# Chunk-selected attention and a softplus layer on one core: the steps in another fixed list

## The chip, the cores and the metric

The kernel runs on one core of a Trainium2 chip. The metric is the device time in microseconds (us) of one execution. Engines: TensorE (PE; its weight loads are PEld), VectorE (DVE), ScalarE (ACT), GpSimd (POOL) and SyncE (SP, which issues most DMAs). Each works through its own instructions strictly in the order of the program, and waits where an input or a buffer is not ready.

## The reference

```python
k_chunks = k.reshape(B, H, nc, chunk, D)             # B=4, H=8, S=768, D=64, chunk=32, nc=24
k_min, k_max = k_chunks.min(3), k_chunks.max(3)
ub = sum_d(max(q * k_min, q * k_max))                # a bound for every query and chunk
ub = where(causal, ub, -1e9); top_chunks = argsort(ub)[..., -6:]
scores = q @ k.T / sqrt(D); masked to the six chosen chunks and to earlier positions
x = (softmax(scores) @ v) as [3072, 512]             # 4 batches of 768 tokens
out = softplus(x @ w_in) @ w_out                     # w_in [512, 2048], w_out [2048, 512]
```

## The kernel before

Everything is one list of 1344 steps, a string called `ORDER`. A loop over it calls one small function for each word, and each function issues its instructions at once, so the list fixes the order on every engine and on every DMA queue; nothing reorders it. A letter at a word's end (V, A, G) says whether VectorE, ScalarE or GpSimd does that copy or sum.

The attention is cut into 20 units of two heads. Units 0 to 3 are the four head pairs of batch 0 for its first 384 tokens, units 4 to 7 the same pairs for its other 384, units 8 to 19 the pairs of batches 1 to 3 with all 768 tokens. The words of a unit u, in the order in which they depend on each other:

- loads: `bk`, `bq`, `bv` (batch 0, in pieces), `Lk`, `Lq`, `Lv` (a whole pair); casts to bf16: `hk`, `hq`, `hv` and `ck`, `cq`, `cv`, `cr`
- transposes of k and q: `kt`, `qt` on TensorE for batch 0 (lines 295, 302), `fk`, `fq` by DMA for the others (line 286)
- selection: `rg` the least and greatest k of a chunk (two, line 309), `pk` packs them into a table (line 314), `qp`, `qn` the positive and negative part of q (lines 328, 330, 335), `U` the bounds (TensorE, lines 345 and 346), `Ua` adds the causal mask, `M` finds the eight greatest (lines 352, 359), `T` writes the row of the choice (two instructions, lines 367 and 368)
- `a` or `s` turns that row on TensorE (lines 376, 387), `ac` or `sc` copies it beside q into `Qaug` (lines 381, 391); `kr`, `qr` put k and q into `Kaug`, `Qaug` (lines 318, 322)
- `S` scores (line 426, `S8.1.2` is unit 8, head 1, third group of columns), `E` exponential on ScalarE (line 432), `D` the causal triangle on GpSimd (line 437), `V` the sum over the values (line 453), `n` divides (lines 463 to 469), `X`, `x` turn the result into `xT` (lines 475, 485)

The layer behind it works on halves of 384 tokens: `I` (line 495) multiplies by `w_in`, `P` is the softplus (line 499). The second product is `F` (line 507) for batch 0; for the others a block scheme with seven products: `g` forms sums of activations (line 551), `m` multiplies (line 565), `e` adds into the output (lines 573 to 585). `t` forms the sums of weights that the scheme needs (line 541), `w` loads the weights. `ob`, `O`, `o` write out. `spin` is a product of zeros whose result nobody reads (line 197); `tE` and `tP` are a one-row activation that makes ScalarE load the table of the exponential or of the softplus.

Buffers are few: two tiles of PSUM each for scores, `I` and `spin` (`ps_big`), for `ub`, turned rows and results (`ps_sm`), and for `kt`, `qt`, `F`, `m` (`ps_w`). Loaded q, k and v have two tiles each. A step that takes the third tile waits until the first has been read.

Of the kernel before, what the change touches and what calls it, by code (L numbers as in the profile page):

```python
# [34 lines left out]
kt4 spin2 X3 x3.V x2.A kr5.0.A I0.0.2.1 I0.0.2.0 P0.0.2 pk5.1.G w2 I0.0.3.1 U5 qt4 I0.0.3.0 hk1.1.G P0.0.3 I0.0.1.0
I0.0.1.1 P0.0.1 qp4.V rg4.0 rg4.1 pk4.0.V qn4 pk4.1.G U4 I0.0.0.1 I0.0.0.0 tP P0.0.0 kr4.0.V kr4.1.V cau1 kt6 kt7 Ua5
kr6.0.A I0.0.4.0 I0.0.4.1 I0.0.5.1 I0.0.5.0 P0.0.4 P0.0.5 kr7.0.V Ua4 M4 rg6.0 T4 rg7.0 rg6.1 pk6.0.V rg7.1 kr6.1.V
pk6.1.V I0.0.6.0 I0.0.6.1 a4.1 I0.0.7.1 I0.0.7.0 ac4.1.A P0.0.6 bv1.0.2 bq1.1.0 bq1.1.1 Lq9 bv1.0.1 Lk8 bv1.1.0
bv1.0.0 bv1.1.2 bv1.1.1 P0.0.7 hq1.1.V qt6 M5 kr7.1.V T5 a5.0 ac5.0.V a4.0 S4.1.1 qn6 qp6.V ac4.0.V a5.1 qt7 zs0
# [10 lines left out]
tP F0.5.0 F0.5.1 S8.0.0 F0.3.0 S8.1.1 F0.3.1 F0.5.2 F0.3.2 F0.3.3 E8.1.1 E8.0.0 S8.1.2 E8.1.2 F0.3.4 S8.0.2 F0.5.3 s9  # L50
S8.1.0 rg10.1 qp10.V sc9.0.V qp11.V pk11.1.A cv11.A pk10.0.A E8.1.0 E8.0.2 kr11.0.G kr10.0.G qr10.0.G kr10.1.V cv8.A
D8.0 pk11.0.G pk10.1.G qr10.1.G Lk12 Lk13 D8.1 F0.5.4 F0.5.5 F0.3.5 U10 sc9.1.V qn11 Ua10 M10 S8.0.1 F0.5.6 S9.0.1
E8.0.1 U11 V8.1 S9.0.0 T10 n8.1 Ua11 M11 E9.0.1 E9.0.0 F0.5.7 S9.1.0 F0.3.6 ob0.5.A E9.1.0 s10 S9.1.1 F0.3.7 V8.0
S9.0.2 E9.1.1 E9.0.2 ck12.G kr11.1.G T11 n8.0 sc10.0.V sc10.1.V qr11.0.G qr11.1.G ck13.G F0.2.0 S9.1.2 F0.2.1 s11
# [604 lines left out]
```

## Time and profile before

| | |
|---|---|
| median of 3 runs | 262.48 us (261.29 to 262.59) |
| profiled execution | 263.69 us, its span from first to last instruction 262.0 us |
| PE busy | 246.1 us, 94% of the span |
| DVE busy | 183.5 us, 70% |
| ACT busy | 176.4 us, 67% |
| POOL busy | 122.5 us, 47% |
| mean granted TensorE clock | 0.986 of full speed |

PE is the engine to look at first, since it is nearly always busy; what a change of order can win is the time in which PE stands still or works at a lower clock. A busy share of 70% does not say that an engine is idle in every stage, so the shares have to be read by stretches.

### The profile page before, as it was taken

Reading aid. Unit: us, or ns where it says so; the run is one execution under the profiler, and the core shown is the slowest. Engines: PE = TensorE matmul, PEld = TensorE weight load, DVE = VectorE, ACT = ScalarE, POOL = GpSimd, SP = SyncE. Lnnn points to the kernel's source line nnn. Section 1 sums busy time; section 2 is a strip of 40 time slices with the busy share of each in tenths; the row PEclk is TensorE's granted clock in tenths of the full one; section 3 lists DMA queues with packets and bytes.
Section 4 is the critical chain, followed back from the end, with each engine's and each line's share of the span. In section 5 each row is a group of like instructions: output and inputs, shape, how many; then the busy total and the mean of one; then the engine's idle time right before and its main releaser. Section 6 shows DMA issues by size and latency. Waiting matters only on the chain.

```text
span 262.0 us, 6544 instructions
## 1 busy us (share of the span) xinstructions
PE 246.1 (94%) x2576; PEld 176.0 (67%) x2576; DVE 183.5 (70%) x553; ACT 176.4 (67%) x236; POOL 122.5 (47%) x148
## 2 busy tenths in 40 slices
PE   7568998999998989999999999999999999999994
PEld 2247665775654657666688888756688887668883
DVE  4877588436798998799999997419787782012593
ACT  5557857996769978866798798967576742662300
POOL 4655513592636983724667575203089910018000
PEclk9977999999999999999999999999999999999999
DMA  6999998859999979889999969994724234200212
GB/s 150 219 193 178 223 195 171 134 75 236 184 207 226 163 153 189 194 130 244 216 241 213 182 143 146 234 190 82 161 42 93 83 75 99 80 4 0 80 63 100
DMA packets 119903, 39.23 MB, mean 150 GB/s; under 512 B 113728, under 2 KB 115776, under 8 KB 119872
## 3 DMA queue, kind: packets, MB, share of 16 engines
q1 hardware_dynamic: 116736, 34.62, 68.2%
q0 software_dynamic: 3136, 4.19, 9.6%
q8 instruction: 20, 0.33, 0.5%
q14 instruction: 11, 0.09, 0.1%
HBM read 27.26 MB, written 6.29 MB: 128 GB/s over the span
## 4 chain that ended last, share of the span: by engine, by line
PE 71%; DVE 12%; ACT 6%; DMA 4%; POOL 3%; issue 2%; SPq 1%; ACTq 0%; POOLq 0%; DVEq 0%
PE hp L495 26%; PE op L565 21%; PE sc L426 11%; PE o_ps L453 6%; DMA qf<-in_q_dram 4%; ACT attnT L432 3%; PE op L507 3%; DVE km L309 2%; DVE m L359 2%; POOL attnT L437 1%; PE spin L197 1%; DVE row L368 1%; ACT Kaug L222 1%; DVE vaug L269 1%; DVE Kaug L318 1%
## 5 line engine op out<-in xcount | busy, mean ns | idle before, releaser
L432 ACT ACTIVATE attnT<-sc 128x1024 bf16<-128x1024 f32 (+3 forms) x96 | 84.1, 917 | 16.0 <-PE sc L426 14.5
L495 PE MATMUL hp<-xT,w_in_sb 128*128 128x384 bf16 x512 | 86.9, 326 | 0.0
L499 ACT ACTIVATE gT<-hp 128x768 bf16<-128x768 f32 x64 | 51.8, 810 | 39.1 <-PE hp L495 39.0
L495 PEld LDWEIGHTS <-w_in_sb 128*128 128x128 bf16 x512 | 49.3, 98 | 31.0 <-issue 0.2
L426 PE MATMUL sc<-Qaug,Kaug 128*128 128x128 bf16 (+3 forms) x400 | 51.9, 259 | 2.6 <-ACT Qaug L381 1.3
L437 POOL TENSOR_SCALAR_AFFINE_SELECT attnT<-attnT 128x768 bf16<-128x768 bf16 (+1 forms) x40 | 31.2, 781 | 26.8 <-ACT attnT L432 24.4
L426 PEld LDWEIGHTS <-Kaug 128*128 128x128 bf16 x400 | 29.9, 99 | 13.4 <-issue 3.8
L565 PEld LDWEIGHTS <-gT 128*128 128x128 bf16 x288 | 27.4, 98 | 5.4 <-DVE ob L579 0.7
L309 DVE TENSOR_REDUCE km<-kT_sb 128x24 bf16<-128x768 bf16 x24 | 22.3, 945 | 10.1 <-DMA kT_sb<-kb 10.1
L565 PE MATMUL op<-w_out_sb,gT 128*128 128x256 f16 x216 | 28.8, 272 | 0.0
L453 PE MATMUL o_ps<-vaug,attnT 128*128 128x65 bf16 x672 | 26.7, 194 | 1.4 <-DVE vaug L269 1.3
L453 PEld LDWEIGHTS <-attnT 128*128 128x128 bf16 x672 | 25.1, 98 | 4.2 <-issue 1.8
L507 PE MATMUL op<-w_out_sb,gT 128*128 128x512 f16 x96 | 26.4, 379 | 0.0
L551 DVE TENSOR_TENSOR mixa<-gT 128x1024 bf16<-128x1024 bf16 x7 | 6.9, 981 | 14.5 <-ACT gT L499 14.4
L359 DVE MAX8 m<-ubm 128x8 f32<-128x8 f32 (+4 forms) x192 | 16.4, 159 | 0.5
L318 POOL COPY Kaug<-kT_sb 64x768 bf16<-64x768 bf16 x17 | 14.4, 855 | 4.2 <-DMA kT_sb<-kb 3.3
L551 POOL TENSOR_TENSOR mixb<-gT,mixa 128x1024 bf16<-128x1024 bf16 x2 | 4.4, 2222 | 24.1 <-DVE mixa L551 24.0
L469 DVE TENSOR_TENSOR on<-o_ps,rr 128x384 bf16<-128x384 f32 x24 | 13.4, 557 | 0.8
L197 PE MATMUL spin<-zeros 128*128 128x512 bf16 x32 | 11.2, 489 | 1.5 <-DVE zeros L194 1.3
L507 PEld LDWEIGHTS <-gT 128*128 128x128 bf16 x96 | 8.4, 98 | 4.5
L352 DVE TENSOR_TENSOR ubm<-ub,causal 128x288 f32<-128x288 f32 (+2 forms) x20 | 7.6, 378 | 3.8 <-PE ub L346 3.3
L314 POOL COPY kmm<-km 64x48 bf16<-64x48 bf16 (+1 forms) x15 | 3.6, 237 | 14.2 <-DVE km L309 13.0
(116 smaller groups left out, 368.4 us busy)
## 6 DMA issues: line engine op xcount, KB each, us to landing
out_dram<-ob SPq DMA_DIRECT2D x24, 256.0 KB, 2.5
qf<-in_q_dram SPq DMA_DIRECT2D x12, 384.0 KB, 4.7
kf<-in_k_dram SPq DMA_DIRECT2D x12, 384.0 KB, 4.8
vf<-in_v_dram SPq DMA_DIRECT2D x12, 384.0 KB, 4.9
...
```

Of the source, the lines that this page charges most:

```text
L197: PE.matmul(o, state[0]["zeros"][:, 0:128], state[0]["zeros"], start=True, stop=True)
L309: V.tensor_reduce(st["km2"][:, which, :], st["kT"].rearrange("d (c t g) -> d c t g", t=4, g=CH // 4), axis=AX.XY, op=(ALU.max, ALU.min)[wh ...
L318: COPY[eng](Ka(p, e)[D * (1 - e):D * (2 - e), t0 * 128:t1 * 128], st["kT"][e * D:(e + 1) * D, :])
L359: V.max(out=st["m8"][:, t, e, :], in_=st["ubm"][:, t, 0:max(8, 4 * (t0 + t + 1)), e])
L426: PE.matmul(sc[:, o:o + (z - a) * 128], Ka(p, e)[:, tj * 128:(tj + 1) * 128], Qa(p, e)[:, a * 128:z * 128], start=True, stop=True)
L432: A.activation(st["at", e][:, g * 1024:g * 1024 + n], st["sc", e, g][:, 0:n], ACT.Exp, scale=scale)
L437: G.affine_select(out=d, in_=d, compare_op=ALU.is_ge, fill=0.0, base=0, channel_multiplier=-1, pattern=[[0, n], [1, 128]])
L453: PE.matmul(o[:, t, :], st["at", e][:, a:a + 128], va[:, tj, e, :], start=(tj == 0), stop=(tj == t0 + t))
L495: PE.matmul(hps[b, h, s][:, n, 0:HALF], w_in_sb[:, dt, ft * 128:(ft + 1) * 128], xT[b][:, dt, h * HALF:(h + 1) * HALF], start=(dt == 0), s ...
L499: A.activation(gT[b, h][:, 2 * s:2 * s + 2, :], hps.pop((b, h, s))[:, :, 0:HALF], ACT.Softplus)
L507: PE.matmul(held[b, t], g[:, ft, c:c + 128], w_out_sb[:, ft, :], start=(ft == 0), stop=(ft == KFF - 1))
L565: PE.matmul(o, x[:, f], y[:, f], start=(f == 0), stop=(f == KH - 1))
```

## The change

Only `ORDER` is replaced. Both lists hold the same 1344 steps with the same units and sizes. The steps stand in other places, and 115 copies, casts and sums go to another engine than before: nine casts of loaded tensors leave ACT for DVE or POOL, and ten of the `g` sums go from POOL to DVE while five go the other way. Among the steps that run behind the first `I` of batch 1, DVE receives the casts `ck17`, `cv12`, `cv13` and `cr15`, the copies `kr17.0` and `kr17.1`, the sums `g4.1.0` and `g4.1.1`, the eviction `e1.1.0` and some small copies (`pk`, `qp`); it gives away `cr17`, `kr15.0`, `t3.0`, `g1.1.1` and some small copies, and `t1.0` stands earlier. The diff is 88 lines of names; its start and the places that are spoken of below:

```diff
-spin9 ident rm0.V bk0.0.1 augb bk0.0.0 bk0.0.2 hk0.0.V cau0 augm kt0 bk1.0.1 bq0.0.2 bq0.0.1 bq0.0.0 bq0.1.2 ar0.1.A
...
-kr3.1.V ac0.1.A S0.1.0 E0.1.0 a0.0 kt2 Ua1 M1 T1 kr2.1.A ac0.0.A qp2.V D0.1 ar2.1.G w0 a1.1 S0.0.0 a1.0 qt3 rg2.0
...
-P0.1.1 I0.1.3.0 I0.1.3.1 P0.1.3 I0.1.0.1 I0.1.0.0 pk9.0.A P0.1.0 kr8.0.G ck10.G kr8.1.G qn9 qp8.V kr9.1.V cq10.V
...
-S10.0.0 E9.1.2 ob0.3.A Lq13 Lv9 cv9.V D9.1 cq13.G D9.0 t1.1.G Lv10 F0.2.2 S10.0.1 E10.0.0 sc11.0.V V9.1 sc11.1.V
...
+spin9 bk0.0.1 bk0.0.2 bk0.0.0 augb augm ar3.1.G kmm spin2 rm0.G ar0.0.A rm1.V ident vones ar3.0.G bq0.0.2 bq0.0.1
...
+bk1.1.1 bq1.0.1 bv0.0.1 bq1.0.0 bk1.0.0 bq1.0.2 bq1.1.0 bk1.0.1 bv0.1.1 bk1.1.0 qt2 U1 a0.0 spin2 S0.1.0 qp2.A ac0.0.A
+kr3.1.V Ua1 M1 T1 kt2 S0.0.0 qn2 ar2.0.V E0.1.0 D0.1 ar2.1.G w0 a1.1 a1.0 qt3 spin2 rg2.1 ac1.0.A E0.0.0 ac1.1.A
+pk3.0.A rg2.0 pk2.1.A pk3.1.A D0.0 hv0.0.0.G S1.1.0 qp3.V kr2.0.V pk2.0.V U2 qn3 U3 spin2 spin2 Ua2 Ua3 M2 hq1.0.V T2
...
+pk9.0.A P0.1.0 I0.1.2.1 I0.1.2.0 Lq10 P0.1.2 tP ob0.1.A cq10.A I0.1.4.1 I0.1.4.0 P0.1.4 qr9.0.G qr9.1.G qr8.1.G Ua8 M8
...
+M11 T11 S9.1.0 ob0.5.A E9.0.0 E9.1.0 V8.0 S9.1.1 F0.2.0 S9.0.2 F0.2.1 F0.2.2 E9.1.1 Lv9 D9.1 sc10.1.V cv9.V n8.0
```

ScalarE, units 0 to 3 of batch 0, from the first copy of a turned row (`ac0.1`) on. Before:

```order
L381 COPY Qaug_97<-qa 128x384
L432 ACTIVATE attnT<-sc 128x768
L318 COPY Kaug_93<-kT 64x384
L381 COPY Qaug_96<-qa 128x384
L432 ACTIVATE attnT<-sc 128x768
L245 CAST vaug_110<-vf 128x6x64
L314 COPY kmm_107<-km_312 64x2x12
L381 COPY Qaug_98<-qa 128x384
```

The same engine in the changed kernel, from the same copy on:

```order
L381 COPY Qaug_97<-qa 128x384
L222 COPY Kaug_90<-aug 64x768
L328 ACTIVATE qpos<-qT 128x384
L381 COPY Qaug_96<-qa 128x384
L432 ACTIVATE attnT<-sc 128x768
L381 COPY Qaug_98<-qa 128x384
L432 ACTIVATE attnT<-sc 128x768
L381 COPY Qaug_99<-qa 128x384
```

The copy into `Qaug_96` (`ac0.0`) now stands before the first exponential (`E0.1.0`) instead of behind it, and the copies of unit 1 (`Qaug_98`, `Qaug_99`) stand around the second.

VectorE, the selection of unit 8, from a `kr` copy on. Before:

```order
L318 COPY Kaug_91<-kT_sb 64x768
L266 CAST qb<-qf 128x768
L352 TENSOR_TENSOR ubm<-ub,causal 128x288
L359 MAX m_1359<-ubm 128x8 x12
L367 TENSOR_TENSOR row_113<-m_1359,minus 128x12
L368 TENSOR_TENSOR row_113<-ubm,m_1359 128x12x24
```

In the changed kernel:

```order
L318 COPY Kaug_90<-kT_sb 64x768
L309 TENSOR_REDUCE km_1327<-kT_sb 128x24 x2
L314 COPY kmm_105<-km_1327 64x48
L352 TENSOR_TENSOR ubm<-ub,causal 128x288
L359 MAX m_1367<-ubm 128x8 x12
L309 TENSOR_REDUCE km_1380<-kT_sb 128x24
L367 TENSOR_TENSOR row_113<-m_1367,minus 128x12
L368 TENSOR_TENSOR row_113<-ubm,m_1367 128x12x24
```

The cast of unit 10's q (`cq10`, line 266) has left this place; it is done by ACT now. One half of unit 10's `rg` stands between `M8` and `T8`.

GpSimd, from the triangle of unit 9 (`D9.1`) to the cast of unit 10's v (`cv10`). Before:

```order
L437 AFFINE_SELECT attnT<-attnT 128x768
L266 CAST qb<-qf 128x768
L437 AFFINE_SELECT attnT<-attnT 128x768
L541 TENSOR_TENSOR mixed_117<-w_out_sb 128x1024
L437 AFFINE_SELECT attnT<-attnT 128x768
L269 CAST vaug_109<-vf 128x12x64
```

In the changed kernel:

```order
L322 COPY Qaug_103<-qT_sb 64x768
L437 AFFINE_SELECT attnT<-attnT 128x768 x2
L322 COPY Qaug_102<-qT_sb 64x768
L437 AFFINE_SELECT attnT<-attnT 128x768
L269 CAST vaug_109<-vf 128x12x64
```

The sum of weights (`t1.1`, line 541) is no longer on GpSimd here; VectorE does it earlier.

## Rows read from the trace of the kernel before

**Rows 1.** The page, its head: span, and each engine's busy time.
```profile
span 262.0 us, 6544 instructions
PE 246.1 (94%) x2576; PEld 176.0 (67%) x2576; DVE 183.5 (70%) x553; ACT 176.4 (67%) x236; POOL 122.5 (47%) x148
```

**Rows 2.** Stretches: length; us busy of PE, PEld, DVE, ACT, POOL; clock; DMA.
```profile
0.00:30.00 30.00, 22.02 (x210) 13.50 (x210) 21.89 (x90) 18.25 (x32) 17.28 (x38) 0.89 1.01 188
30.00:100.00 70.00, 65.91 (x713) 43.01 (x714) 52.69 (x181) 56.07 (x74) 37.84 (x52) 1.00 1.03 174
100.00:250.00 150.00, 150.00 (x1583) 112.63 (x1582) 102.19 (x272) 102.07 (x132) 67.41 (x60) 1.00 0.67 135
250.00:262.00 12.00, 8.20 (x74) 6.88 (x71) 6.78 (x13) 0.00 (x0) 0.00 (x0) 0.98 0.24 89
```

**Rows 3.** The same view between the changes of the granted clock.
```profile
9.02:12.44 3.42, 1.65 (x26) 0.98 (x23) 2.77 (x19) 2.01 (x4) 2.27 (x9) 1.00 1.11 226
12.44:15.85 3.41, 2.96 (x18) 1.74 (x16) 3.30 (x16) 0.49 (x2) 1.73 (x3) 0.50 1.27 221
15.85:19.26 3.41, 1.36 (x20) 1.06 (x18) 1.98 (x8) 2.78 (x5) 2.43 (x4) 1.00 1.18 192
19.26:22.68 3.42, 3.01 (x39) 2.61 (x40) 2.93 (x20) 2.33 (x6) 2.79 (x5) 0.50 0.86 122
```

**Rows 4.** Instructions in order of time, first 30 us; brackets: idle before, its releaser.
```profile
15.84 0.81 ACT L432 ACTIVATE attnT<-sc 128x768 bf16<-128x768 f32 x1 [1.87 <-PE sc L426]
...
17.70 0.49 PE L426 MATMUL sc<-Qaug,Kaug 128*128 128x128 bf16 x5 [1.31 <-ACT Qaug L381]
...
18.23 0.81 ACT L432 ACTIVATE attnT<-sc 128x768 bf16<-128x768 f32 x1 [0.58 <-PE sc L426]
...
18.94 0.51 ACT L245 CAST vaug<-vf 128x384 bf16<-128x384 f32 x1
...
22.23 0.82 PE L197 MATMUL spin<-zeros 128*128 128x512 bf16 x2
...
25.11 3.06 ACT L432 ACTIVATE attnT<-sc 128x768 bf16<-128x768 f32 x4
```

**Rows 5.** Instructions in order of time, 92 to 95 us.
```profile
92.29 2.12 POOL L541 TENSOR_TENSOR mixed<-w_out_sb 128x1024 f16<-128x1024 f16 x1
...
92.60 2.23 DVE L269 CAST vaug<-vf 128x768 bf16<-128x768 f32 x1
...
94.88 0.81 PE L453 MATMUL o_ps<-vaug,attnT 128*128 128x65 bf16 x21 [1.29 <-DVE vaug L269]
```

**Rows 6.** Instructions in order of time, 61 to 80 us.
```profile
61.10 0.83 ACT L266 CAST qb<-qf 128x768 bf16<-128x768 f32 x1 [1.43 <-DMA qf<-in_q_dram]
...
62.36 0.33 PE L475 MATMUL x_ps<-ident,on 128*128 128x128 bf16 x3 [0.41 <-ACT xT L485]
...
71.79 0.56 DVE L266 CAST qb<-qf 128x768 bf16<-128x768 f32 x1 [0.67 <-DMA qf<-in_q_dram]
...
74.39 0.51 PE L387 MATMUL sT<-ident,row 128*128 128x128 bf16 x6 [0.48 <-DVE row L368]
...
77.82 1.28 ACT L432 ACT_TABLE_LOAD   x1 [1.30 <-PE sc L426]
```

**Rows 7.** Groups by line and shape: busy us, mean ns of one, idle before.
```profile
L437 POOL TENSOR_SCALAR_AFFINE_SELECT attnT<-attnT 128x768 bf16<-128x768 bf16 x24 | 22.7, 949 | 16.8 <-ACT attnT L432 14.5 <-issue 1.8 <-ACT dummy L200 0.4
...
L318 DVE COPY Kaug<-kT_sb 64x768 bf16<-64x768 bf16 x7 | 3.0, 428 | 0.2
...
L266 DVE CAST qb<-qf 128x768 bf16<-128x768 f32 x5 | 2.8, 559 | 0.9 <-DMA qf<-in_q_dram 0.9
...
L551 DVE TENSOR_TENSOR mixd<-gT,mixb 128x1024 bf16<-128x1024 bf16 x5 | 4.0, 810 | 0.1
...
L551 POOL TENSOR_TENSOR mixd<-gT,mixb 128x1024 bf16<-128x1024 bf16 x4 | 8.8, 2198 | 1.5 <-issue 1.5
```

**Rows 8.** Busy time by stretches, 110 to 160 us.
```profile
110.00:160.00 50.00, 50.00 (x563) 37.91 (x561) 46.27 (x153) 40.95 (x55) 29.84 (x30) 1.00 0.95 189
```

More of the change, by code (lines that the diff above doesn't have):

```diff
@@ L35 @@
[L35 to L39, printed above, removed]
@@ L50 @@
[L50 to L54, printed above, removed]
@@ L105 @@
-g3.3.2.V g4.3.2.V m2.3.2.0 m2.3.2.1 m6.3.2.0 m6.3.2.1 m5.3.2.0 m5.3.2.1 m7.3.2.0 m7.3.2.1 e2.3.2 e3.3.2 e4.3.2
-m3.3.2.0 m3.3.2.1 e6.3.2 o3.2.0 m4.3.2.0 m4.3.2.1 e7.3.2 o3.2.1
+spin9 bk0.0.1 bk0.0.2 bk0.0.0 augb augm ar3.1.G kmm spin2 rm0.G ar0.0.A rm1.V ident vones ar3.0.G bq0.0.2 bq0.0.1
+bq0.0.0 bv0.1.0 bk0.1.2 bv0.0.0 bk0.1.0 bk0.1.1 bq0.1.0 bq0.1.1 bq0.1.2 hk0.0.V kt0 kt1 kr0.1.V rg0.1 rg0.0 hq0.0.A
+kr0.0.A cau0 ar0.1.G pk0.1.G spin7 hk0.1.G hq0.1.G cau1 pk0.0.V kr1.0.V kr1.1.V rg1.0 qt0 qp0.V qn0 qt1 U0 rg1.1 Ua0
@@ new lines @@
+M0 T0 kt3 rg3.0 qp1.V qn1 rg3.1 a0.1 kr3.0.V pk1.1.A pk1.0.A ar1.1.A ac0.1.A ar1.0.A bv0.0.2 bv0.1.2 bk1.0.2 bk1.1.2
+bk1.1.1 bq1.0.1 bv0.0.1 bq1.0.0 bk1.0.0 bq1.0.2 bq1.1.0 bk1.0.1 bv0.1.1 bk1.1.0 qt2 U1 a0.0 spin2 S0.1.0 qp2.A ac0.0.A
+kr3.1.V Ua1 M1 T1 kt2 S0.0.0 qn2 ar2.0.V E0.1.0 D0.1 ar2.1.G w0 a1.1 a1.0 qt3 spin2 rg2.1 ac1.0.A E0.0.0 ac1.1.A
+pk3.0.A rg2.0 pk2.1.A pk3.1.A D0.0 hv0.0.0.G S1.1.0 qp3.V kr2.0.V pk2.0.V U2 qn3 U3 spin2 spin2 Ua2 Ua3 M2 hq1.0.V T2
+M3 S1.0.0 V0.0 V0.1 a2.1 E1.1.0 kr2.1.A E1.0.0 ac2.1.V hk1.0.G a2.0 qt4 S2.1.0 n0 X0 T3 ac2.0.A E2.1.0 hv0.1.1.A
@@ new lines @@
+hv0.0.1.A w1 D1.0 hv0.1.0.A D1.1 D2.1 qn4 a3.1 x0.V qp4.V S2.0.0 kt4 ac3.1.V kr4.1.V a3.0 qt5 V1.0 S3.1.0 ac3.0.V
+rg4.0 rg4.1 E2.0.0 V2.1 V1.1 n1 S3.0.0 D2.0 E3.1.0 E3.0.0 V2.0 D3.1 qn5 n2 kr4.0.V X1 spin2 V3.1 qp5.A x1.V D3.0
+hk1.1.G pk4.1.G w2 V3.0 kt5 spin2 X2 n3 X3 x2.V x3.V kt6 spin2 I0.0.1.1 pk4.0.V I0.0.1.0 P0.0.1 kr5.0.A I0.0.0.0 U4
+I0.0.0.1 tP rg6.1 Ua4 rg6.0 rg5.0 rg5.1 pk5.0.V P0.0.0 pk5.1.G kr5.1.V I0.0.2.0 I0.0.2.1 I0.0.3.1 I0.0.3.0 kt7 U5
+rg7.1 rg7.0 kr7.0.V P0.0.2 P0.0.3 I0.0.5.0 I0.0.5.1 Ua5 M4 kr7.1.V T4 M5 P0.0.5 kr6.0.A I0.0.4.1 I0.0.4.0 T5 kr6.1.V
@@ new lines @@
+I0.0.7.1 I0.0.7.0 P0.0.4 pk6.1.A I0.0.6.0 I0.0.6.1 P0.0.7 P0.0.6 bv1.0.2 bq1.1.2 bq1.1.1 Lk8 Lq9 bv1.0.1 bv1.0.0
+bv1.1.2 bv1.1.0 bv1.1.1 a5.0 a4.1 ac4.1.V ac5.0.V pk7.1.G hq1.1.G pk6.0.G qt6 qt7 a5.1 a4.0 S4.1.1 S5.0.0 qn7 qp6.V
+ac4.0.V qn6 U6 zs0 pk7.0.G w3 E4.1.1 E5.0.0 F0.1.0 F0.1.1 S4.0.0 Ua6 M6 qp7.V U7 Ua7 T6 ac5.1.V F0.1.2 S4.0.1
+hv1.0.0.V F0.1.3 E4.0.0 E4.0.1 S4.1.0 a6.1 a6.0 F0.0.0 S5.0.1 E4.1.0 D4.0 hv1.0.1.G D4.1 D5.0 M7 ac6.1.V T7 ac6.0.V
+V4.0 S6.1.1 a7.0 V4.1 E5.0.1 S6.1.0 F0.0.1 E6.1.1 ac7.0.V E6.1.0 D6.1 hv1.1.0.G S5.1.0 n4 X4 x4.V E5.1.0 D5.1 ck8.G
@@ new lines @@
+V5.0 S6.0.0 a7.1 ac7.1.V F0.0.2 S5.1.1 V6.1 E6.0.0 E5.1.1 fk8 S7.0.0 F0.0.3 E7.0.0 Lq8 S6.0.1 V5.1 E6.0.1 S7.0.1
+F0.1.4 D6.0 S7.1.0 E7.0.1 E7.1.0 zs1 cq9.G D7.0 D7.1 Lk9 ck9.G kr8.1.G kr8.0.G n5 X5 hv1.1.1.V x5.V V6.0 n6 rg8.1
+S7.1.1 F0.1.5 E7.1.1 tE cq8.A V7.0 F0.1.6 V7.1 n7 F0.0.4 F0.1.7 F0.0.5 X7 X6 F0.0.6 F0.0.7 Lk10 fq9 fq8 fk9 Lk11 x7.V
+ck10.G x6.A I0.1.1.1 I0.1.1.0 P0.1.1 I0.1.7.0 I0.1.7.1 I0.1.3.0 I0.1.3.1 P0.1.7 I0.1.5.1 qp8.A rg8.0 pk8.1.G pk8.0.G
+qn8 I0.1.5.0 U8 P0.1.3 qp9.A fk10 ck11.G kr9.1.V qr8.0.V kr9.0.V I0.1.0.0 I0.1.0.1 rg9.1 rg9.0 pk9.1.V P0.1.5 ob0.0.A
@@ new lines @@
+pk9.0.A P0.1.0 I0.1.2.1 I0.1.2.0 Lq10 P0.1.2 tP ob0.1.A cq10.A I0.1.4.1 I0.1.4.0 P0.1.4 qr9.0.G qr9.1.G qr8.1.G Ua8 M8
+rg10.0 T8 Lq11 I0.1.6.1 s8 I0.1.6.0 fk11 Lv11 rg10.1 qn9 F0.5.0 U9 F0.3.0 F0.3.1 sc8.1.V sc8.0.V S8.0.0 kr11.0.V
+rg11.0 rg11.1 Ua9 fq10 cq11.G pk10.1.G Lv8 fq11 P0.1.6 E8.0.0 F0.5.1 S8.1.1 E8.1.1 F0.5.2 F0.3.2 F0.5.3 S8.1.2 S8.1.0
+pk10.0.G E8.1.2 kr11.1.G D8.0 F0.3.3 F0.5.4 S8.0.2 F0.5.5 M9 E8.1.0 D8.1 cv8.A E8.0.2 pk11.0.A qp11.A kr10.1.G cv11.G
+Lk12 ck12.G pk11.1.G Lk13 ck13.G qr10.1.G qr11.1.G qp10.V T9 s9 qn10 kr10.0.V qr10.0.V t1.1.V sc9.0.V sc9.1.V qn11
@@ L107 @@
+m1.3.0.1 g1.3.0.V g2.3.0.V g1.3.2.V g4.3.0.V g3.3.0.V e1.3.0.A m1.3.2.0 m1.3.2.1 e1.3.2.A m2.3.0.0 m2.3.0.1 m6.3.0.0
+m6.3.0.1 m5.3.0.0 m5.3.0.1 m7.3.0.0 e2.3.0 m7.3.0.1 e3.3.0 e4.3.0 m3.3.0.0 m3.3.0.1 m4.3.0.0 m4.3.0.1 g2.3.2.V
+g3.3.2.V e5.3.0 o3.0.0 o3.0.1 m2.3.2.0 m2.3.2.1 m6.3.2.0 m6.3.2.1 m5.3.2.0 m5.3.2.1 e2.3.2 m7.3.2.0 m7.3.2.1 e3.3.2
+e4.3.2 g4.3.2.G m3.3.2.0 m3.3.2.1 e6.3.2 o3.2.0 m4.3.2.0 m4.3.2.1 tE tP e7.3.2 o3.2.1
 """
```

115 lines of the change are left out of this document (49 added, 66 removed).

## The prediction, made before the changed kernel ran

> **What bounds the kernel now.** First the page's head [rows 1]: PE is busy 246.1 of 262.0 us, so all that another order can win is 15.9 us of idle PE and what PE loses at half clock. Then the busy time by stretches, cut where the behaviour changes [rows 2]. PE's idle time is 8.0 us in the first 30, 4.1 us in the next 70, nothing in the 150 us that follow, and 3.8 us in the last 12. The reader is to see that the long middle cannot become shorter: there PE waits for nobody, and both lists give it the same products. The last 12 us hold the last evictions and the last store, whose steps stand in the same order in both lists but for two idle table loads. So the change can win in the first 100 us only, and behind that it can only lose.
>
> The same view between the changes of clock [rows 3] shows a second cost: the granted clock is 0.50 from 12.44 to 15.85 and from 19.26 to 22.68, the 1.2 GHz level; each of the two came behind a stretch in which PE was busy 1.65 and 1.36 us of 3.4. Last, the instructions in order of time show who ends PE's waits: in the first 30 us a chain through DVE and ACT [rows 4], from 61 to 80 a load and DVE's selection [rows 6], at 93 a cast [rows 5].
>
> DVE's cast of unit 9's v at 92.60 took 2.23 us where such a cast takes 0.56 [rows 5, 7]. GpSimd's 2.12 us sum had begun at 92.29; the cast ended 0.42 us behind it. This is GpSimd's hold on DVE, which the new list counts. The Trainium skill ("SBUF — State Buffer", section "SBUF: two separate sides") says of it that whichever of the two begins first has the shared ports for its whole instruction and the other "fully blocks". By that rule the cast would have stood from 92.60 to 94.41 and ended at 94.97; it ended at 94.83, so the trace agrees to within 0.14 us.
>
> **The start (to 30 us).** The new list turns the selection so that both heads of unit 0 score before unit 1 is chosen. In the list before, the score of head 0 waits 1.31 us for a copy of ACT that stands behind the first exponential and begins at 17.70; its exponential begins at 18.23 [rows 4]. Now that copy stands before the first exponential. That one I leave at 15.84: the product ahead of it waits for the turn of a later q and a spin at half clock. Then the score of head 0 follows at once, at about 16.0, and its exponential waits only for ACT: 15.84 + 0.81 for the first, a copy of 0.5, so 17.3, 0.9 us earlier. From there on the gain can be lost again. Before the second score of unit 1 the new list has four spins where the old one had none; two spins took 0.82 us at half clock [rows 4], so four take 1.64, and 0.82 at full clock. Behind this score ACT works off an exponential, a copy, another exponential, three casts of v (0.51 each [rows 4]) and the last three exponentials. Working through these, the last exponential of unit 3 ends at about 27.3 if the clock is full there and at 28.4 if it is half; now it ends at 25.11 + 3.06 = 28.17 [rows 4]. That is -0.9 or +0.2; I take -0.3. Two further turns (`qt4`, `kt6`, three products each; three of this size take 0.33 us [rows 6], less where they follow close on others) now lie in this idle start and no longer in the dense stretch behind 30 us: -0.3 for both. Term: -0.6, bounds -1.2 and +0.2.
>
> **From 30 to 100 us.** Four waits of PE change here.
> - Before `X7` it waits 0.41 us for a copy on ACT, queued behind a cast that waited 1.43 us for its load [rows 6]. One of the two copies is on DVE now, and two `F` stand between `X6` and the next `I`: -0.4, bounds -0.5 and 0.
> - Before `s8` it waits 0.48 us for DVE's row [rows 6]. DVE had waited 0.67 us in the cast of unit 10's q with the selection of unit 8 queued behind it. That cast is on ACT now. Its load is issued one transpose later (`fk10` stands ahead of `Lq10` on SP), so ACT may wait in it with `P0.1.4` behind; PE has some 2.9 us of `I`, `F` and `U` before it needs that buffer. But one `rg10` of 0.94 us, which needs `fk10`, stands inside the selection. -0.5, bounds -0.5 and +0.5.
> - At 77.82 ACT loads the exponential's table only when the score has come, 1.28 us [rows 6]. Both lists put `tE` or `tP` where it doesn't help here, and PE waits for the first two exponentials of unit 8 in both: 0, bounds -0.9 and 0.
> - Before `V9.1` it waits 1.29 us for the held cast [rows 5]. The 2.12 us sum is off GpSimd at this place; a triangle of 0.95 us or a copy may be in its place [rows 7], and one more `F` of 0.43 us covers: -1.0, bounds -1.3 and 0.
>
> Term: -1.9. All four hang on loads which GpSimd's casts trigger; those casts move with the exponentials, so an earlier start moves them along.
>
> **From 100 us on.** Here only a loss is possible, and DVE is the engine to look at. In 110 to 160 us it is busy 46.27 of 50 [rows 8], 3.7 spare. What it receives there: four casts of 0.56, two `kr` of 0.43, two sums of 0.81 [rows 7], 4.7 us; what it gives away or did earlier: a cast, a `kr` and three sums, 3.4 us. With an eviction and some `pk` more, about 1 us, it has 2.4 us more to do. The six casts and sums are of the kinds that GpSimd holds. At 0.3 us of hold each the stretch is over-filled by 2.4 + 1.8 - 3.7 = 0.5 us, which PE then waits. Without any hold nothing is lost; the bound above is the second rival. GpSimd has fewer long sums in the new list, which speaks for little. Term: +0.5, bounds 0 and +8.7.
>
> Moves that I cost at nothing: copies that change engine in the stretch behind 168 us, where PE is at 10.0 of 10 and DVE is less loaded (102.19 us of 150 in the whole stretch [rows 2]); if their cover went, each costs its 0.4 to 0.8 us once. The sum `g4.3.2` near the end goes from DVE, 0.81, to GpSimd, 2.20 [rows 7]; four `m` stand on PE between its input and its reader and cover the 1.4 us more, all of which PE would wait without them. The two table loads at ScalarE's end stand behind its last copy, while PE has products for several us.
>
> Sum: -0.6 - 1.9 + 0.5 = -2.0. The profiled execution took 263.69 us, 1.7 over its span of 262.0 and 1.2 over the median of 262.48; its waits are taken as those of a median run, so 262.5 - 2.0 = 260.5 us.
>
> **Rivals.** *The clock falls elsewhere, and nothing is won.* The list counts on five phases of the clock. The new start has PE idle longer around 9 to 12 us, and fewer spins behind it, so the stretch from 15.85 to 19.26, now at full clock [rows 3], may be at half. Between the first score of unit 0 and the last of unit 1 PE has 3.2 us of work at full clock in the new list; at half clock it is 6.4. If half of the 3.2 us is on the path, the start's -0.6 becomes +1.0, and the loads and casts behind it come later, too: about 262.3. For it speaks that the two phases at half clock followed stretches with little PE work; against it that ACT's chain, not PE, ends this stretch. The Trainium skill ("TensorE: Matmul & The Clock Gate", Part 1) speaks against a list with fixed phases: it says that the switch is not tied to the kernel's start and differs from run to run. The runs shown spread by 1.3 us, which does not decide it.
>
> *DVE becomes the bound behind 110 us, and it is slower.* Place: the casts and sums that DVE receives there. If each of the six stands behind one triangle of GpSimd, 0.95 us [rows 7], DVE has 2.4 + 5.7 - 3.7 = 4.4 us too much, and PE, which has no idle time there to give, waits as long: 262.5 - 2.5 + 4.4 = 264.4. It decides from 3.8 us of overflow on, that is six holds of 0.85. At the 1.67 us that the cast at 92.60 lost it would be 8.7 us. Against it: DVE has more room before 110 and behind 160, and its steps can run late where their readers are far behind.
>
> *All four waits go and the start gains 1.2 us*: 262.5 - 1.2 - 0.5 - 0.5 - 0.9 - 1.3 = 258.1.
>
> **How the numbers follow.** Something within 0.5%, 1.3 us, cannot be told from no change here. The forecast, 258.9 to 261.1, gets 0.53; all gains, 0.06; no change through the clock, 0.25; slower through DVE, 0.16. The predicted time is the first one's, 260.5. The range from 258.0 to 264.0 takes in the full gain and most of the second rival. Faster by over 0.5%: 0.53 + 0.06 = 0.59; same 0.25; slower 0.16.
>
> **What would show it.** In the changed kernel's profile: the score of head 0 starting near 16 us and the last exponential of unit 3 ending between 27.3 and 28.4; PE's idle time of 30 to 100 us near 2 to 2.5 instead of 4.1; the cast of unit 9's v under 1.2 us; and 150 us of PE without idle time behind 100. It would be wrong if PE is granted half clock behind 22.7 us, if PE shows idle time released by DVE between 110 and 168 us, or if the last exponential of unit 3 ends behind 28.6 us.

## The result, and the profile after

The changed kernel took 265.31 us (264.78 to 265.77, 4 runs), the kernel before 262.53 beside it: ratio 1.0121, 95% interval 1.0076 to 1.0166. It is slower by 2.8 us where 2.0 us faster was forecast. All ratios here compare undisturbed runs alone; medians of the kernel before lay between 262.5 and 264.5 us from one comparison to the next, so kernels are compared by ratio. The profiled execution took 264.78 us. The page's head, then the stretches of [rows 2] and [rows 8], with the same columns:

```profile
span 263.1 us, 6559 instructions
PE 246.0 (94%) x2576; PEld 175.0 (67%) x2576; DVE 181.6 (69%) x557; ACT 177.4 (67%) x234; POOL 118.5 (45%) x148
```

```profile
0.00:30.00 30.00, 22.66 (x225) 13.51 (x226) 25.40 (x96) 18.32 (x32) 18.68 (x39) 1.00 1.08 199
30.00:100.00 70.00, 66.37 (x735) 43.97 (x734) 50.61 (x178) 56.70 (x74) 38.99 (x53) 1.00 1.03 175
100.00:250.00 150.00, 147.64 (x1539) 109.79 (x1538) 98.40 (x272) 100.38 (x126) 58.45 (x56) 1.00 0.72 133
...
110.00:160.00 50.00, 48.95 (x550) 36.82 (x549) 47.13 (x153) 39.65 (x50) 26.30 (x27) 1.00 1.09 197
```

PE's idle time is 7.3 us in the first 30, 3.6 in the next 70, and 2.4 in the 150 us where there was none. The clock is full throughout, in the first 30 us too, where [rows 3] had two stretches at half. The other three executions of the changed kernel had a mean granted clock of 0.986 to 0.994, so in this the profiled one is not typical.

Idle time leaves out what half clock costs, so the tables below use another sum. In dense stretches a product of 256 columns starts 0.107 us behind the last, which is 2.4 columns per ns; with 26 ns for the smallest ones, of 24 or 48 columns, as they follow each other in the traces, all products of the program make 231.0 us. The time at which so many us of products have begun, less these us, is what PE has **lost** by then. Steps stand at other times in two lists, so this compares equal work.

| lost, us | to 30 us of products | 30 to 100 | 100 to the end |
|---|---|---|---|
| before, the profiled execution | 17.10 | 6.24 | 4.06 |
| changed | 15.57 | 5.44 | 7.50 |
| difference | -1.5 | -0.8 | +3.4 |
| forecast | -0.6 | -1.9 | +0.5 |

### The profile page after: what moved, and what is told of

It is laid out like the page before. It is cut to its first block, busy times and chain, and to the rows that moved or that the text cites. A ratio compares the mean times of both kernels' runs of the same rounds, so it can differ in the third digit from the quotient of the medians.

```text
span 263.1 us, 6559 instructions
## 1 busy us (share of the span) xinstructions
PE 246.0 (94%) x2576; PEld 175.0 (67%) x2576; DVE 181.6 (69%) x557; ACT 177.4 (67%) x234; POOL 118.5 (45%) x148
## 4 chain that ended last, share of the span: by engine, by line
PE 61%; DVE 19%; DMA 8%; ACT 3%; issue 3%; POOL 2%; SPq 2%; POOLq 0%; ACTq 0%; DVEq 0%
PE hp L495 28%; PE op L565 15%; PE sc L426 8%; PE o_ps L453 4%; DVE km L309 4%; PE op L507 3%; DMA Qaug<-row 3%; ACT attnT L432 3%; DVE m L359 2%; SPq L230 2%; DMA xT<-on 2%; DMA kT_sb<-kb 2%; DMA kf<-in_k_dram 1%; DVE Kaug L318 1%; PE qa L376 1%
## 5 line engine op out<-in xcount | busy, mean ns | idle before, releaser
L426 PE MATMUL sc<-Qaug,Kaug 128*128 128x128 bf16 (+3 forms) x400 | 51.0, 255 | 3.4 <-ACT attnT L432 1.2
L437 POOL TENSOR_SCALAR_AFFINE_SELECT attnT<-attnT 128x768 bf16<-128x768 bf16 (+1 forms) x40 | 32.1, 807 | 35.1 <-ACT attnT L432 32.8
L551 POOL TENSOR_TENSOR mixd<-gT,mixb 128x1024 bf16<-128x1024 bf16 x4 | 9.1, 2266 | 52.6 <-DVE mixb L551 38.6
L565 PEld LDWEIGHTS <-gT 128*128 128x128 bf16 x288 | 27.3, 98 | 5.4 <-DVE ob L579 0.7
L551 DVE TENSOR_TENSOR mixa<-gT 128x1024 bf16<-128x1024 bf16 x8 | 6.2, 769 | 15.4 <-ACT gT L499 15.4
L266 POOL CAST kb<-kf 128x768 bf16<-128x768 f32 x10 | 8.8, 881 | 12.5 <-DMA kf<-in_k_dram 12.3
L318 POOL COPY Kaug<-kT_sb 64x768 bf16<-64x768 bf16 x13 | 11.2, 863 | 3.9 <-DMA kT_sb<-kb 3.2
L581 DVE TENSOR_TENSOR ob<-op,ob 128x512 f32<-128x512 f32 x8 | 5.5, 688 | 9.0 <-PE op L565 9.0
```

Of the source, the lines that this page charges most:

```text
L318: COPY[eng](Ka(p, e)[D * (1 - e):D * (2 - e), t0 * 128:t1 * 128], st["kT"][e * D:(e + 1) * D, :])
L426: PE.matmul(sc[:, o:o + (z - a) * 128], Ka(p, e)[:, tj * 128:(tj + 1) * 128], Qa(p, e)[:, a * 128:z * 128], start=True, stop=True)
L437: G.affine_select(out=d, in_=d, compare_op=ALU.is_ge, fill=0.0, base=0, channel_multiplier=-1, pattern=[[0, n], [1, 128]])
L551: TT[eng](s[k], x, y, op=ALU.subtract)
L565: PE.matmul(o, x[:, f], y[:, f], start=(f == 0), stop=(f == KH - 1))
```

## The experiments

**Thirds of the two lists.** The lists hold nearly the same steps up to step 312 (46 us), and up to step 622 of the new one and 620 of the old (about 99 us). A kernel takes one list up to a cut and then the steps that are left in the order of the other; in the names, a is the new list and b the one before.

```diff
-ORDER = new
+ORDER = new[:312] + rest_of(old)                  # a_b_b; a_a_b cuts at 622
+ORDER = old[:312] + rest_of(new)                  # b_a_a; b_b_a cuts at 620
```

a_b_b: 

> The first 312 steps from the new list (to about 46 us), everything behind them in the order of the list before. Theory (the loss lies behind 100 us, where VectorE got more to do): this kernel has only the start of the new list, whose PE waits in the two profiles sum to 14.1 us up to the first score of unit 4, against 15.7 before, so it should be 1.5 us faster than before, near 261.0. Rival (the start loses through the clock): the profiled run of the changed kernel had full clock everywhere, three others 0.986 to 0.994 and up to 1 us more; then the new start is at 263 or more.

b_a_a: 

> The reverse: the first 312 steps of the list before, the rest of the new one. Theory: the gain of the start is gone and the loss behind 100 us stays, 265.3 + 1.5 = 266.8. Rival (the start's clock is the loss): faster than the changed kernel, 263 or less.

a_a_b: 

> The new list to about 99 us (622 steps), behind it the steps that are left in the order of the list before. Theory: both gains stay and the loss of 3.3 us behind 100 us is gone: 262.5 - 1.5 - 0.6 = 260.4. Rival (the loss behind 100 us is only what comes late out of the first part, loads and casts that the new start triggers at other times): 263 or more, with the same waits behind 130 us.

b_b_a: 

> The list before to about 99 us (620 steps), behind it the new list. Theory: 262.5 + 3.3 = 265.8, with waits of PE at the scores of units 12 and 17 and at the bounds of unit 17. Rival (it comes late out of the first part): 262 to 263, and no such waits.

**The kernel before again**, for a trace at another clock:

> The kernel before, unchanged, for one more trace of it. Theory (the profiled execution of before lost 1.9 us in its start to two stretches at half clock, which other executions do not have): if the clock is full in the first 30 us, it has lost 15.3 us when 30 us of products are done, as b_a_a with the same start, and ends near 261.8. Rival (the start of b_a_a is quick for another reason): 17 us lost there in spite of full clock.

| kernel | ratio to before, 95% interval | lost to 30 | 30 to 100 | 100 to end |
|---|---|---|---|---|
| before_again | (one run, 262.04 us) | 15.27 | 5.64 | 4.84 |
| a_b_b | 1.0118, 1.0072 to 1.0164 | 17.19 | 5.96 | 7.55 |
| b_a_a | 0.9990, 0.9944 to 1.0036 | 15.25 | 3.94 | 6.50 |
| a_a_b | 1.0119, 1.0053 to 1.0186 | 16.37 | 7.02 | 4.57 |
| b_b_a | 1.0160, 1.0110 to 1.0210 | 15.91 | 8.20 | 6.59 |

The column on the right tells of the end: with the new end 6.5 to 7.5 us are lost behind 100 us, with the old end 4.1 to 4.8. Two kernels with the old end lost more there, a_b_b (7.6) and b_a_b (9.2); both are taken up below.

But the times do not follow the end. In three of the four kernels they came out on the side of the rival: a_b_b and a_a_b, with the new start and the old end, are as slow as the changed kernel (1.0118 and 1.0119 against 1.0121), and b_a_a, with the old start and the new end, has lost nothing (0.9990). Only b_b_a went as its theory said, and 2.0 us of its loss are a wait at its seam. The row of a_a_b is from the fastest of its six executions, 264.21 us where their median is 267.33, so it does not show what held up the others. The new start acts further on: the middle of the new list loses 3.9 us behind the old start and 5.4 to 7.0 behind the new one, and the changed kernel lost 0.3, 1.5 and 1.0 us more than b_a_a in the three columns.

The column on the left tells of the start. Stretches of before_again (columns as in [rows 3]):

```profile
12.44:15.85 3.41, 2.20 (x21) 1.46 (x22) 3.24 (x17) 1.93 (x4) 2.16 (x4) 1.00 1.35 221
19.26:22.68 3.42, 1.81 (x24) 1.30 (x23) 3.32 (x15) 1.76 (x4) 2.58 (x5) 1.00 1.08 195
```

At full clock the same list lost 15.27 us where the profiled execution had lost 17.10. The new start, at full clock too, lost 15.57. Full clock is rare with the new start: eight of the ten traces with it have half clock between 10.9 and 19.2 us and lost 16.2 to 17.2 us in this column, and of all its executions on record 2 of 78 had a mean clock of 0.996 or more, against 57 of 178 with the old start. Scores and exponentials of units 0 to 3 in order of time, in before_again and then in the changed kernel:

```profile
14.35 0.81 ACT L432 ACTIVATE attnT<-sc 128x768 bf16<-128x768 f32 x1 [0.72 <-PE sc L426]
...
16.22 0.49 PE L426 MATMUL sc<-Qaug,Kaug 128*128 128x128 bf16 x5 [0.37 <-ACT Qaug L381]
...
16.75 0.81 ACT L432 ACTIVATE attnT<-sc 128x768 bf16<-128x768 f32 x1 [0.58 <-PE sc L426]
...
23.26 3.06 ACT L432 ACTIVATE attnT<-sc 128x768 bf16<-128x768 f32 x4
```

```profile
14.34 0.50 PE L426 MATMUL sc<-Qaug,Kaug 128*128 128x128 bf16 x5
14.38 0.81 ACT L432 ACTIVATE attnT<-sc 128x768 bf16<-128x768 f32 x1 [0.20 <-PE sc L426]
...
16.14 0.82 ACT L432 ACTIVATE attnT<-sc 128x768 bf16<-128x768 f32 x1
...
24.03 2.29 ACT L432 ACTIVATE attnT<-sc 128x768 bf16<-128x768 f32 x3 [0.31 <-PE o_ps L453]
```

The score of head 0 starts 1.9 us earlier in the new list and its exponential 0.6, as the change says. Yet the last exponential of unit 3 ends at 26.32 in both (23.26 + 3.06, 24.03 + 2.29): the gain is gone within units 1 to 3.

**The new wait between 60 and 80 us.** One copy goes to GpSimd:

```diff
-pk9.0.A P0.1.0 I0.1.2.1
+pk9.0.G P0.1.0 I0.1.2.1
```

> The changed kernel with one copy, pk9.0, on GpSimd instead of ScalarE. On ScalarE it waits 2.06 us for the reduction of unit 9's k, with the softplus P0.1.0 queued behind, and PE waits 1.89 us for the buffer that this softplus frees. Theory (that queue is the new wait that took back the gain between 60 and 80 us): the 1.89 us go down to 0.3 or less, 265.3 - 1.5 = 263.8. Rival (the softplus is late for other reasons, or PE then waits as long at s8 for the row of unit 8): 265.0 or more.

Measured: 1.0103 (1.0067 to 1.0139), no gain. In the changed kernel this copy waits on ScalarE for a reduction of unit 9's k, which VectorE begins late because the transpose of that k lands late:

```profile
62.79 1.24 SPq L286 DMA_TRANSPOSE kT_sb<-kb  x1
...
67.42 0.35 DVE L318 COPY Kaug<-kT_sb 64x768 bf16<-64x768 bf16 x1 [2.50 <-DMA kT_sb<-kb]
...
70.28 0.25 ACT L314 COPY kmm<-km 64x48 bf16<-64x48 bf16 x1 [2.06 <-DVE km L309]
...
71.26 2.11 PE L495 MATMUL hp<-xT,w_in_sb 128*128 128x384 bf16 x12 [1.73 <-ACT gT L499]
```

In pk9_g PE waits earlier, for unit 8's q, whose transpose was late there (3.7 us behind the end of its issue, 1.8 in the changed kernel):

```profile
68.23 0.84 ACT L328 ACTIVATE qpos<-qT_sb 128x768 bf16<-128x768 bf16 x1 [2.17 <-DMA qT_sb<-qb]
...
69.13 0.20 PE L345 MATMUL ub<-kmm,qpos 128*128 128x48 bf16 x1 [1.31 <-ACT qpos L328]
```

In both traces a late transpose ends the wait; the queue on ScalarE is where it showed. In b_a_a, with the same steps from 46 us on, this part of the trace reads:

```profile
62.09 1.24 SPq L286 DMA_TRANSPOSE kT_sb<-kb  x1
...
65.31 0.36 DVE L318 COPY Kaug<-kT_sb 64x768 bf16<-64x768 bf16 x1 [0.27 <-DMA kT_sb<-kb]
```

From the end of its issue this transpose took 3.4 us to land in the changed kernel (67.4 less 64.03) and 2.0 in b_a_a (65.3 less 63.33). It took 3.2 to 3.6 in six more kernels with the new start and the same order here, and 2.0 in three of four more with the old start.

**Who does the copies behind 100 us.** tail_letters gives 53 steps behind step 622 back to their old engines and keeps the new order; unit17 does so for three:

```diff
-pk17.1.V pk17.0.V E15.1.2 ... T16 g2.1.2.V kr17.0.V n14.1
+pk17.1.G pk17.0.G E15.1.2 ... T16 g2.1.2.V kr17.0.G n14.1
```

> The new list's order; behind about 99 us (step 622) the 53 copies, casts and sums that differ go to the engines of the list before. Theory (the loss behind 100 us is the work that VectorE received): at equal products done PE loses 7.5 us behind 100 us in the changed kernel and 4.1 before; here about 5, so 265.3 - 2.5 = 262.8. Rival (the order of the steps behind 100 us makes VectorE late, whoever does the copies): 265 or more, and the long sums that go back to GpSimd hold VectorE besides.

> The changed kernel with three copies of unit 17 back on GpSimd: pk17.0, pk17.1 and kr17.0, which took 0.76, 0.88 and 1.02 us on VectorE (1.9 us of it hold) ahead of unit 17's mask and maxima. Theory: PE's 0.78 us before the bounds of unit 17 and 1.20 us before its first score go: 265.3 - 1.8 = 263.5. Rival (VectorE's later steps are late through their order, not through these three): both waits keep over half of their size.

tail_letters: 1.0780 (1.0715 to 1.0845), 283.95 us; it lost 22.7 us behind 100. Its rows show what the old engines do in the new order:

```profile
137.97 0.95 DVE L309 TENSOR_REDUCE km<-kT_sb 128x24 bf16<-128x768 bf16 x1 [5.88 <-DMA kT_sb<-kb]
...
139.58 1.35 PE L565 MATMUL op<-mixed,mixb 128*128 128x256 f16 x8 [3.30 <-DVE mixb L551]
...
144.14 2.55 POOL L551 TENSOR_TENSOR mixd<-gT,mixb 128x1024 bf16<-128x1024 bf16 x1
...
146.75 1.05 PE L565 MATMUL op<-w_out_sb,mixd 128*128 128x256 f16 x8 [1.30 <-POOL mixd L551]
```

The first wait of PE, 3.30 us, is for a sum on VectorE that stands behind a reduction, and this one waited 5.88 us for a transpose whose cast, `ck16`, ScalarE now does behind its softplus. The second, 1.30, is for a sum on GpSimd; two more such waits, of 1.89 and 1.29, follow behind 200 us. So the new order cannot go without the letters that came with it. Whether the work that VectorE received is itself a part of the loss, this run does not tell. unit17: 1.0066 (1.0035 to 1.0097), an interval that overlaps the changed kernel's. The 0.61 us before unit 17's bounds went; the wait at its first score stayed at 0.89, and one of 0.48 came at unit 16's.

**Loads ahead of transposes.**

```diff
-F0.0.7 Lk10 fq9 fq8 fk9 Lk11 ... Lv14 Lq16 fs12.1 fs12.0 ... fs16.1 Lv18 S15.0.2 ... fs17.0 Lv16
+F0.0.7 fq9 fq8 fk9 Lk10 Lk11 ... Lv14 fs12.1 fs12.0 Lq16 ... fs16.1 S15.0.2 ... fs17.0 Lv18 Lv16
```

That is loads_behind, and b_a_a_loads with the old start. lv18_late and b_a_a_lv18 move Lq16 as here, leave Lk10, and put Lv18 behind fx15.

> The changed kernel with three loads of 384 KB issued behind the DMA transposes that they stood ahead of on SP: Lk10 behind fk9, Lq16 behind fs12.0, Lv18 behind fs17.0. In the trace of the changed kernel SP's transfers land in the order of their issue, and fs12.1 and fs17.0 land 0.7 and 0.8 us behind the load ahead of them, fq9 0.9 us behind Lk10. Theory (these loads make the transposes late, and the transposes make PE wait): the 1.89 us before I0.1.4.1 go to under 0.5 and the 1.20 us before S17.0.0 too; PE's loss between 50 and 70 us of products done goes from 3.75 to about 2.3, between 110 and 140 from 4.1 to about 2.8: 265.3 - 2.7 = 262.6. Rival (VectorE, not the transposes, ends these waits): fs17.0 is issued at VectorE's row anyway and nothing changes behind 100 us, 264 or more.

> b_a_a (start of the list before, the rest of the new one) with the same three loads behind the transposes. b_a_a lost 3.5 us between 110 and 140 us of products done, 1.35 of it before S17.0.0. Theory: that one goes, 1 to 1.5 us less than b_a_a, 261.5 in the median. Rival (VectorE ends these waits): the same as b_a_a, 263.

> The changed kernel with Lq16 behind fs12.0 and Lv18 behind fx15 (the list before has Lv18 even later; its cast stands 170 steps behind). Theory (the loads that the new list issues early on SP's queue are what makes the transposes behind them late): the wait of 1.20 us before S17.0.0 goes, and the 2.36 us before I2.1.4.1 that arose with Lv18 directly behind fs17.0 does not come, since fx15 is now ahead of it too. PE's loss between 110 and 150 us of products done goes from 4.4 to 2.6: 265.3 - 1.8 = 263.5. Rival (VectorE full): a wait of the same size at another score or sum, 265 or more.

> The start of the list before (312 steps), then the new list with the same two loads moved. b_a_a lost 3.8 us between 110 and 150 us of products done. Theory: 2.2 here, so 1.5 us less than b_a_a: 260.3 at full clock, 261.5 in the median. Rival: as b_a_a, 262 at full clock, 263.4 in the median.

loads_behind: 1.0199 (1.0097 to 1.0300). The 1.73 us before `I0.1.4.1` went, but PE waited 1.72 before unit 8's bounds instead. The loss between 110 and 140 us of products fell from 4.1 to 2.3, but a new wait came behind that, since the load now stands ahead of transposes of `xT`:

```profile
171.46 0.97 PE L495 MATMUL hp<-xT,w_in_sb 128*128 128x384 bf16 x5 [2.20 <-DMA xT<-on]
```

b_a_a_loads: 1.0213 (1.0164 to 1.0263), with the same wait. lv18_late: 1.0076 (1.0036 to 1.0115); between 110 and 150 it lost 3.6 instead of 4.4, where 2.6 was expected, and still waited for four transposed rows (0.10 to 0.54). b_a_a_lv18: 1.0000 (0.9953 to 1.0048), like b_a_a. Early loads are at most a part of the loss.

**Slack.** Unit 17 in the changed kernel, its bounds, a copy ahead of its mask, the mask, the transpose of its row and its first score:

```profile
153.01 0.18 PE L345 MATMUL ub<-kmm,qpos 128*128 128x48 bf16 x1 [0.61 <-DVE ubm L352]
...
155.18 1.02 DVE L318 COPY Kaug<-kT_sb 64x768 bf16<-64x768 bf16 x1
...
156.94 0.45 DVE L352 TENSOR_TENSOR ubm<-ub,causal 128x288 f32<-128x288 f32 x1
...
159.50 1.21 SPq L277 DMA_TRANSPOSE Qaug<-row  x1
...
163.38 0.62 PE L426 MATMUL sc<-Qaug,Kaug 128*128 128x128 bf16 x7 [1.04 <-DMA Qaug<-row]
```

and mask, transpose and score in before_again:

```profile
152.82 0.46 DVE L352 TENSOR_TENSOR ubm<-ub,causal 128x288 f32<-128x288 f32 x1 [0.25 <-PE ub L346]
...
156.69 1.24 SPq L277 DMA_TRANSPOSE Qaug<-row  x1
...
161.05 1.05 PE L426 MATMUL sc<-Qaug,Kaug 128*128 128x128 bf16 x14
```

There VectorE waits for the bounds. Here the mask starts 3.6 us after the last product of the bounds has begun (153.29), behind a row, a sum, `kr17.0` and a division. For four of the sixteen rows that are turned by DMA, the time from the landing of the transpose to the first score that reads it:

| us of slack | S12.1.0 | S14.1.2 | S15.0.1 | S17.0.0 |
|---|---|---|---|---|
| before_again | 7.0 | 7.0 | 2.3 | 0.2 |
| changed | 0.0 | 0.0 | 0.3 | 0.0 |

(In the list before, the first score of S14.1.2's row is `S14.1.0`.) Other rows gained slack, that of `S19.0.2` from 1.5 to 4.3. Of the four, PE waited in the changed kernel's trace 1.04 us for the last, 0.10 for the second and not at all for the others; the rest of its 2.4 us of idle time are the 0.61 before unit 17's bounds, 0.34 before `S12.0.0` and 0.28 before an `I`.

s17_later moves one score and its exponential behind three products; b_a_a_s17 does the same with the old start.

```diff
-S17.0.0 m5.1.2.0 m5.1.2.1 E17.0.0 ... m7.1.2.0 S16.1.1
+m5.1.2.0 m5.1.2.1 ... m7.1.2.0 S17.0.0 E17.0.0 S16.1.1
```

> The changed kernel with one score and its exponential, S17.0.0 and E17.0.0, behind three products m5.1.2.0, m5.1.2.1 and m7.1.2.0 (0.43 us each) instead of ahead of them. In the changed kernel the transposed row of unit 17 lands at 163.3 and its first score starts at 163.4, without slack, behind a wait of 1.20 us; in before_again it lands 0.2 us early and PE doesn't wait. Theory (the new order leaves no slack between a row's transpose and its score): the three products cover 1.2 us, the wait goes to 0.1 or less and PE loses 1.1 us less between 130 and 140 us of products done: 264.2 in the median. Rival (VectorE or ScalarE is late at this place whatever PE does): the wait turns up before S16.1.1, m7.1.2.1 or S16.1.2, 265.0 or more.

> The same two steps moved in b_a_a, where this score waited 1.35 us. Theory: 1.2 us less than b_a_a, 260.8 at full clock, 262.2 in the median. Rival: as b_a_a.

In both the wait is gone: between 130 and 140 us of products 0.7 and 0.4 us were lost instead of 1.6 and 1.8. s17_later still took 1.0090 (1.0052 to 1.0128), and gave the gain back where `xT` is read:

```profile
171.69 0.97 PE L495 MATMUL hp<-xT,w_in_sb 128*128 128x384 bf16 x5 [1.80 <-DMA xT<-on]
```

b_a_a_s17 took 0.9988 (0.9952 to 1.0023); its trace lost 25.2 us in all, that of b_a_a 25.7.

**GpSimd's hold, and a better list.** a_b_b has the old end and yet lost 7.6 us in it. Two sums on GpSimd began just ahead of two rows of the choice; in the kernel before the first row began ahead of the sum and stood only behind a triangle. First a_b_b, then the kernel before:

```profile
134.86 2.12 POOL L551 TENSOR_TENSOR mixd<-gT,mixb 128x1024 bf16<-128x1024 bf16 x1
...
135.00 2.05 DVE L367 TENSOR_TENSOR row<-m,minus 128x12 bf16<-128x12 f32 x1
...
138.89 1.03 PE L565 MATMUL op<-w_out_sb,mixd 128*128 128x256 f16 x8 [1.12 <-DVE ob L575]
```

```profile
134.22 0.86 POOL L437 TENSOR_SCALAR_AFFINE_SELECT attnT<-attnT 128x768 bf16<-128x768 bf16 x1 [0.28 <-ACT attnT L432]
...
134.69 0.46 DVE L367 TENSOR_TENSOR row<-m,minus 128x12 bf16<-128x12 f32 x1
...
135.06 2.41 POOL L551 TENSOR_TENSOR mixd<-gT,mixb 128x1024 bf16<-128x1024 bf16 x1
```

abb_g4 is a_b_b with both sums on VectorE; b_a_b has the new list from step 312 to 622 only; b_a_b_g4 is b_a_b with both sums on VectorE, the first right behind its row:

```diff
-T14 rg16.0 ... g4.1.0.G ... g4.1.1.G
+T14 g4.1.0.V rg16.0 ... g4.1.1.V
```

> The kernel a_b_b (start of the new list, then the list before) with two sums, g4.1.0 and g4.1.1, on VectorE instead of GpSimd. In a_b_b each began on GpSimd just ahead of a row of the choice (T14, T15), which then took 2.38 and 2.31 us, 0.79 and 0.55 in the kernel before, and PE waited 1.28 and 1.44 us for the evictions behind them. Theory (hold by whichever begins first): both rows are back under 0.9 us, the two waits go, 266.1 - 2.3 = 263.8. Rival (the rows are long for another reason, or VectorE is full there and the two sums of 0.7 us take the same time): 265.5 or more.

> The list before to step 312, the new list to step 622, the list before behind that. If the three parts add up at equal products done: the start as in b_a_a (15.25 us lost at 30 us of products), the middle as there (3.9), the end as before (4.1 to 4.6), so 2.0 us less than b_a_a's 25.7: about 260.0 at full clock and 261.0 in the median, 1.5 below the kernel before. Rival (the order of the end only works from the times at which the middle of its own list leaves VectorE and the loads, as a_b_b and b_b_a showed at their seams): 263 or more.

> b_a_b (before, new from step 312 to 622, before) with two sums off GpSimd: g4.1.0 on VectorE right behind T14, g4.1.1 on VectorE where it stood. The profile of b_a_b had T14 and T15 at 2.1 and 2.2 us, each begun just behind one of these sums, and waits of 1.29 and 1.45 us behind them; its fastest runs of 260.1 us are taken as those without this. Theory: the rows take 0.55 us in every run, loss between 110 and 130 us of products 1.5 instead of 4.2, and the median is 260.5. Rival (VectorE is so full there that 1.4 us of sums cost PE as much): 262 or more.

abb_g4: 1.0047 (1.0010 to 1.0084). The instruction of 2.05 us took 0.21; but the first sum, behind a second row on VectorE, then made PE wait 1.86. By ratio 1.9 of the 2.3 us expected came, though its interval overlaps that of a_b_b; in the traces it lost 0.7 us less behind 100. b_a_b: 0.9968 (0.9929 to 1.0008); its trace, of an execution of 266.83 us, has both waits of a_b_b again (1.12 and 1.28). b_a_b_g4: 0.9950 (0.9904 to 0.9996), the one list that beat both kernels, though barely clear of no change, which one of so many lists can be by chance, and 1.3 us better by ratio where 2.0 was expected. PE has no idle time in the full stretch of VectorE:

```profile
110.00:160.00 50.00, 50.00 (x579) 38.29 (x578) 45.82 (x154) 40.88 (x54) 25.17 (x28) 1.00 1.10 196
```

It lost 4.2 us between 30 and 100 and 4.3 behind: the new list's middle and the old list's end.

## Why the prediction was wrong

**The start, -0.6.** The score of head 0 was forecast near 16 us and came at 14.34; the last exponential of unit 3 ended at 26.32, earlier than the 27.3 to 28.4 forecast. But that is the clock: before_again ends it at 26.32 as well, and at equal clock the new start lost 0.3 us more (15.57 against 15.27). The step that failed is "its waits are taken as those of a median run": the profiled execution had paid 1.8 us (17.10 less 15.27) for two stretches at half clock, and the wait of 1.31 us [rows 4] that the term removed is 0.37 at full clock. In these two profiles the first rival had the clock's part the wrong way round: half clock was in the profile of before. Over other executions half clock does fall into the new start, as this rival says (eight of ten traces); what that adds to the medians was not separated.

**30 to 100 us, -1.9.** Of the four waits, `X7` and `V9.1` went, since `cv9` was not held:

```profile
90.39 0.56 DVE L269 CAST vaug<-vf 128x768 bf16<-128x768 f32 x1
```

The one at the first exponentials of unit 8 went too, and `s8` kept 0.25 of 0.48. Then the 1.73 us before `I0.1.4.1` took most of it back, and -0.8 came. Behind the old start the middle lost 3.9 in b_a_a, 1.7 less than in before_again, so the term was right there. Two steps failed. "PE has some 2.9 us of `I`, `F` and `U` before it needs that buffer": ScalarE was held earlier than in the cast that the step looked at, at the end of a chain from unit 9's transpose. And "an earlier start moves them along": the new start is not earlier at equal clock, and behind it this transpose was issued 0.7 us later than in b_a_a and landed 2.1 us later.

**From 100 us on, +0.5.** This term missed by most: +3.4 against the profile of before, +2.7 against before_again. The side and the place were those of the second rival; its mechanism was not. VectorE's busy time in 110 to 160 us rose by 0.9 us (46.27 [rows 8] to 47.13), not by 2.4 and six holds, and PE's largest wait behind 100 us is for a transpose (1.04), not for VectorE. The step that failed is "the stretch is over-filled by": it asks whether VectorE has room in 50 us, where the list asks whether a row, its transpose and its score follow each other in time. Four of these chains have almost no slack left. Moving one score removed its wait, which shows that link; it did not make the kernel faster (1.0090, in an interval that overlaps the changed kernel's).

**The sum.** Against before_again the three parts make +0.3 - 0.2 + 2.7 = +2.8 us, the difference of the two spans in the profiles. That the medians differ by as much is in part luck, since they hold executions at other clocks. And the sum adds three terms as if each part ran alike whatever ran ahead of it, which the experiments refute: behind the old start the same middle and end cost nothing (0.9990), behind the new one 1.0121, and the new start alone, with the old rest, 1.0118 (a_b_b; 1.0047 without its two holds, abb_g4). So the exchange of the start makes the difference, though at full clock it loses only 0.3 us itself. The new end is no gain either: behind the old start and middle it lost 6.6 us, where the old end loses 4.1 to 4.8.

**What stays open.** How the new start makes the middle and the end slower. How the loss behind 100 us divides between VectorE's late rows and SP's queue: with one wait taken away another followed, at `xT` above all. And why unit 9's transpose lands 1.4 us later behind the new start. One coincidence bears on that: in all eight traces in which it landed 3.2 us or more after its issue's end, a packet of 16384 bytes on an instruction queue (q8 of the page) began 0.2 to 1.5 us after that end. In the four with 2.0 us it began 1.3 us or more after it, in the seven others only after the landing. No run moved that packet, so it is not shown to be the cause.
